# A 120-row piece of 88 columns half way through the run, moved by two transfers each way in place of five

## The chip, the cores and the metric

The kernel runs on one core of a Trainium2 chip. The metric is the device time of one execution in microseconds, over several executions. One core has no second die to compare with; all runs used here are of the state "fast". Several chips were used, and the kernel before was run again beside every experiment: it took between 477.96 and 481.73 us. Times are compared as ratios to the kernel before on the same chip.

## The reference, cut to what matters

```
x: (1, 512, 512, 192) bf16      w: (1, 1, 4, 48, 48) bf16
out[pixel, g, :] = x[pixel, g, :] @ w[0, 0, g]        # 4 groups of 48 channels
```

This is a grouped 1x1 convolution: 262,144 pixels of 384 bytes go in and as many come out, 201.3 MB in all. Each pixel is multiplied by four 48x48 matrices. There is little arithmetic for each byte.

## The kernel before

Pixels lie in SBUF, the memory on the chip, as columns: a column is one pixel in each of the 128 partitions ("rows"). Loads on the sync queue bring 80 columns at a time into a ring of 240 columns. PE (the matrix engine) transposes, VectorE copies what was transposed, PE multiplies it by the weights, ScalarE copies the result to an output ring of 280 columns, and stores on the scalar queue (q10 in the profile; the loads are q1) carry it out. Four columns are a "group".

The plan reckons with 8 rows for each of the 16 DMA engines in a transfer of 128 rows. The tail of the kernel before bears this out: the one engine that still works there moves eight packets of 6,144 bytes, then eight of 3,072, each packet one row of the last two stores (packet records, 475.4 to 478.2 us). One field of the plan is different: a piece of 120 rows, meant to give 15 engines 8 rows each and one nothing. It is there to relieve one DMA engine. Since 120 rows don't add up to a whole number of 128-row columns, a few columns of 16 rows stand beside it.

```python
FULL = (("sync", 0, 128, 128),)
PARTIAL = (                                   # queue, first row, rows, outer
    ("sync", 0, 16, 4), ("sync", 32, 16, 4),
    ("pool", 52, 44, 11), ("pool", 20, 12, 3), ("pool", 96, 32, 8),
)
REST = (("sync", 0, 16, 4),)
PARTIALS = ((72, PARTIAL), (4, REST))
FRONT_SLOTS = 9
FILL_BEFORE = (2, 3)
...
        # transfers(): a piece that is not of 128 rows
        view = px.rearrange("(c a i) n -> a c (i n)", a=outer, c=rows // outer)
        yield n, view, tile[r0:r0 + rows, at * C:(at + c1 - c0) * C]
...
            # gpsimd: a tiny transfer of 5 rows ("filler") ahead of two of the three blocks
            for p in partial:
                gp.wait_ge(t_done, freed(p))
                for n, dram, sbuf in transfers(xf, ring, p, ("pool",)):
                    filler(n)
                    gp.dma_start(sbuf, dram).then_inc(ld_sem[ld_key[p.i, n]], 16)
```

The outer number is meant to say over how many engines a block is dealt. In the packet records of the kernel before, at most 4 load packets of the 16-row blocks and at most 11 of the gpsimd blocks run at a time. The fillers are meant to keep the gpsimd blocks off the engine that is to be relieved; how they do so, no trace shows, only that one engine is idle beside the piece's store (next section).

## Time and profile before

| | before |
|---|---|
| time, median of the first 3 runs | 479.5 us (479.33 to 479.69) |
| span of the profiled run (first to last instruction) | 479.1 us |
| bytes moved | 201.75 MB, 421 GB/s over the span |
| DMA share (mean busy share of the 16 engines), 10 to 470 us | 0.98 to 1.03 in every 10 us |
| PE busy | 428.6 us |
| end of the DMA engines | 15 of them at 472.9 to 475.3 us, one at 478.2 us |

From the page of the kernel before: the busy time of the compute engines, the busy tenths of the DMA engines in 40 slices, and what they moved in each slice.

```profile
PE 428.6 (89%) x6178; PEld 387.1 (81%) x6178; DVE 246.9 (52%) x258; ACT 388.5 (81%) x515; POOL 7.0 (1%) x18
...
DMA  8999999999999999999999999999999999999995
GB/s 325 442 393 426 430 434 428 429 433 435 435 427 428 430 432 434 424 424 417 432 427 431 433 429 428 428 442 433 426 432 427 438 428 430 437 419 434 423 415 223
```

The DMA engines are full from the second slice to the last but one, at about 430 GB/s. PE is busy for 428.6 us and has slack. DMA is what bounds this kernel.

From the table of stages of the kernel before (the stretch; its length; busy us and count of PE, weight loads, VectorE, ScalarE and gpsimd; PE's granted clock; DMA share; GB/s):

```profile
180.00:190.00 10.00, 1.95 (x18) 1.97 (x19) 0.48 (x1) 0.00 (x0) 0.00 (x0) 0.60 1.02 440
...
230.00:240.00 10.00, 9.90 (x152) 9.02 (x149) 5.75 (x6) 8.82 (x13) 0.00 (x0) 1.00 0.99 417
472.00:475.30 3.30, 0.00 (x0) 0.00 (x0) 0.00 (x0) 0.00 (x0) 0.00 (x0) 0.51 0.49 201
475.30:478.30 3.00, 0.00 (x0) 0.00 (x0) 0.00 (x0) 0.00 (x0) 0.00 (x0) 0.50 0.06 25
```

In the first line PE waits for the 120-row piece and does nearly nothing, but DMA moves 440 GB/s: that wait costs no time. In the last line the DMA share is 0.06, one engine of 16, for 3 us.

From the waits (us in total, times, longest) and from the DMA issues (count, size, us from issue to landing) of the kernel before:

```profile
PE xT_ps L320 <- DMA ring<-in_x_dram: 15.7, 4, 10.4
...
ACT oring L416 <- DMA out_dram<-oring: 12.5, 6, 3.6
```

```profile
ring<-in_x_dram POOLq DMA_DIRECT2D x1, 864.0 KB, 45.7
...
out_dram<-oring POOLq DMA_DIRECT2D x1, 864.0 KB, 41.2
```

The trace also keeps a record of every DMA packet: its queue, its start, its duration and its bytes, though not its engine. Here one packet is one row of a transfer (23 loads of 128 rows and 80 columns left 2944 packets of 30,720 bytes). Packets of one size take the same time nearly always: 1138 ns for 80 columns (30,720 bytes), 1025 ns for 72 columns, 968 ns for 68. The first is 27 GB/s for one engine, the rate that the prediction reckons with. One unbroken chain of packets is slower: between 60 and 440 us its loads take 18 ns more and its stores 61 to 71 ns more. Picked out by their length alone, these are 145 of 2489 loads of 80 columns, about one in 17. Loads and stores together, 194 of the 271 that follow another of the kind begin within 5 ns of its end. So I take this chain for one engine of the 16, 4% slower than the rest over loads and stores together. It is the relieved one: while the piece's store keeps the other engines busy, at 221 to 224 us, 15.1 engines are busy on average in place of 16, and the slow packets are missing from the record just there.

### The profile page before, as it was taken

The page shows a single profiled execution, that of the slowest core. Times are in us where ns is not written, and L with a number is a line of the kernel's source. Part 1 is how long each engine was busy: PE and PEld are TensorE (multiplying, and loading weights), DVE is VectorE, ACT ScalarE, POOL GpSimd, SP SyncE. Part 2 cuts the span into 40 slices and gives each one's busy share as a digit, 9 for nine tenths or more (in the row PEclk, how much of TensorE's full clock was granted, in tenths as well). Part 3 has the DMA queues.
Part 4 walks back from the last instruction along what each step waited for, and adds up shares of the span by engine and source line. Part 5 has one row for each costly group of instructions (what it writes and reads, how often), then busy time and mean ns, then how long its engine had stood idle before and what let it go on. Part 6 is the DMA issues. An engine that isn't in the chain of part 4 may idle for free.

```text
span 479.1 us, 13570 instructions
## 1 busy us (share of the span) xinstructions
PE 428.6 (89%) x6178; PEld 387.1 (81%) x6178; DVE 246.9 (52%) x258; ACT 388.5 (81%) x515; POOL 7.0 (1%) x18
## 2 busy tenths in 40 slices
PE   5999999999999763989998999999999798899980
PEld 4888888888889753878888888888888687888870
DVE  2655556555555440545654555555556355355540
ACT  2998899988999771878898888999888696688881
POOL 1000000000020000020000000000000000000000
PEclk9999999999999995999999999999999899799997
DMA  8999999999999999999999999999999999999995
GB/s 325 442 393 426 430 434 428 429 433 435 435 427 428 430 432 434 424 424 417 432 427 431 433 429 428 428 442 433 426 432 427 438 428 430 437 419 434 423 415 223
DMA packets 9894, 201.75 MB, mean 421 GB/s; under 512 B 1657, under 2 KB 1817, under 8 KB 2457
## 3 DMA queue, kind: packets, MB, share of 16 engines
q1 hardware_dynamic: 4156, 98.25, 48.1%
q10 hardware_dynamic: 5100, 98.23, 48.0%
q0 software_dynamic: 608, 4.87, 2.4%
q8 instruction: 20, 0.33, 0.2%
q14 instruction: 10, 0.07, 0.0%
HBM read 100.68 MB, written 100.66 MB: 420 GB/s over the span
## 4 chain that ended last, share of the span: by engine, by line
PE 55%; DMA 29%; ACT 9%; issue 1%; ACTq 1%; POOL 1%; another core or an unknown queue 1%; SPq 0%
PE o_ps L340 32%; PE xT_ps L320 23%; DMA out_dram<-oring 18%; DMA ring<-in_x_dram 11%; ACT oring L416 9%; ACTq L397 1%; POOL fill L263 0%; POOL ring L270 0%; POOL out_dram L276 0%; SPq L289 0%; SPq L282 0%; ACTq L390 0%; ACTq L399 0%
## 5 line engine op out<-in xcount | busy, mean ns | idle before, releaser
L416 ACT CAST oring<-o_ps 128x768 bf16<-128x768 f32 x514 | 387.2, 801 | 79.7 <-PE o_ps L340 59.7
L379 DVE COPY xT_sb<-xT_ps 128x1536 bf16<-128x1536 bf16 x257 | 246.2, 958 | 215.9 <-PE xT_ps L320 215.9
L340 PE MATMUL o_ps<-wt,xT_sb 128*128 128x144 bf16 (+1 forms) x3084 | 288.2, 235 | 20.7 <-ACT oring L416 15.4
L340 PEld LDWEIGHTS o_ps<-wt,xT_sb 128*128 128x128 bf16 x3084 | 211.3, 99 | 59.2 <-ACT oring L416 49.6
L320 PE MATMUL xT_ps<-ident,ring 128*128 128x128 bf16 x3084 | 221.2, 222 | 15.7 <-DMA ring<-in_x_dram 15.7
L320 PEld LDWEIGHTS xT_ps<-ident,ring 128*128 128x128 bf16 x3084 | 189.2, 99 | 18.4 <-issue 13.9
L263 POOL DMA_DIRECT2D fill<-in_x_dram x4 | 2.4, 597 | 205.6 <-PE xT_ps L320 137.8
L301 PE MATMUL o_ps<-w_sb,esel 48*128 48x48 bf16 x10 | 0.6, 210 | 2.8 <-DMA w_sb<-in_w_dram 2.8
L301 PEld LDWEIGHTS o_ps<-w_sb,esel 48*128 48x128 bf16 x10 | 0.5, 112 | 2.8 <-issue 2.8
L372 DVE CAST wt<-o_ps 128x480 bf16<-128x480 f32 x1 | 0.7, 659 | 3.4 <-PE o_ps L301 3.4
L416 ACT ACT_TABLE_LOAD x1 | 1.3, 1283 | 0.8 <-PEq L436 0.8
L270 POOL DMA_DIRECT2D ring<-in_x_dram x3 | 1.7, 563 | 0.0
L276 POOL DMA_DIRECT2D out_dram<-oring x3 | 1.7, 558 | 0.0
L249 POOL TENSOR_SCALAR_AFFINE_SELECT esel<-esel 48x272 bf16<-48x272 bf16 x1 | 0.4, 404 | 0.0
L246 POOL MEMSET esel<- 48x272 bf16 x1 | 0.3, 318 | 0.3 <-POOLq L436 0.3
L253 POOL TENSOR_SCALAR_AFFINE_SELECT ident<-ident 128x128 bf16<-128x128 bf16 x1 | 0.3, 284 | 0.0
L247 POOL MEMSET ident<- 128x128 bf16 x1 | 0.2, 199 | 0.0
L436 POOL MEMSET const-float32-0.0<- 128x1 f32 x1 | 0.1, 99 | 0.3 <-issue 0.3
L436 POOL MEMSET const-bfloat16-1.0<- 128x1 bf16 x1 | 0.1, 102 | 0.0
L436 POOL MEMSET const-uint8-127<- 128x1 uint8 x1 | 0.1, 102 | 0.0
L436 POOL MEMSET const-float32-1.0<- 128x1 f32 x1 | 0.1, 99 | 0.0
## 6 DMA issues: line engine op xcount, KB each, us to landing
ring<-in_x_dram SPq DMA_DIRECT2D x23, 3840.0 KB, 27.2
out_dram<-oring ACTq DMA_DIRECT2D x13, 3456.0 KB, 40.6
out_dram<-oring ACTq DMA_DIRECT2D x11, 3264.0 KB, 39.3
out_dram<-oring ACTq DMA_DIRECT2D x3, 1344.0 KB, 22.4
out_dram<-oring ACTq DMA_DIRECT2D x2, 1920.0 KB, 21.9
out_dram<-oring ACTq DMA_DIRECT2D x1, 3072.0 KB, 31.8
ring<-in_x_dram SPq DMA_DIRECT2D x1, 2880.0 KB, 19.9
ring<-in_x_dram SPq DMA_DIRECT2D x1, 2304.0 KB, 10.9
```

The lines of the kernel that those rows point to most:

```text
L249: gp.affine_select(out=esel[:], in_=esel[:], pattern=[[-1, ECOLS]], compare_op=AluOpType.is_equal, fill=0.0, base=ESHIFT, channel_multipli ...
L263: gp.dma_start(dst, src).then_inc(fill_sem[k], 16)
L270: gp.dma_start(sbuf, dram).then_inc(ld_sem[ld_key[p.i, n]], 16)
L276: gp.dma_start(dram, sbuf).then_inc(st_sem[i][n], 16)
L301: last = pe.matmul(o_ps[:, NOB - 1, col:col + CG], lhsT=esel[:, s0:s0 + 128], rhs=w_sb[:, g, :], start=True, stop=True, skip_group_check=True)
L320: last = pe.transpose(xT_ps[:, g % NXP, j * 128:(j + 1) * 128], xg[:, j * 128:(j + 1) * 128], ident[:])
L340: last = pe.matmul(o_ps[:, v % NOB, c0_:c1_], lhsT=xs[:, j * 128:(j + 1) * 128], rhs=wt[:, WOFF[tc]:WOFF[tc] + (c1_ - c0_)], start=(tc == ...
L372: dve.tensor_copy(wt[:], o_ps[:, NOB - 1, 0:WCOLS]).then_inc(wc_sem, 1)
L379: dve.tensor_copy(xT_sb[pair % NXS][:, 0:n * 2 * UC].rearrange("p (g c) -> p g c", g=n), xT_ps[:, b0:b0 + n, 0:2 * UC]).then_inc(e_done[pa ...
L397: act.dma_start(dram, sbuf).then_inc(st_sem[i][n], 16)
L416: act.copy(out_columns(g).rearrange("p (u c) -> p u c", u=2), o_ps[:, v % NOB:v % NOB + 2, 0:UC]).then_inc(fa_done[g % (2 * NTOK)] if g < ...
L436: nc = _bacc.Bacc("TRN2", target_bir_lowering=False, num_devices=1)
```

## The change

The intent: give the slow engine still less work (88 columns in place of 72, by which 128-row columns go from 1980 to 1964), put the relief half way through the run, and move the piece by one gpsimd transfer of 88 rows and one of 32 rows on the sync queue (outward: on the scalar queue), in place of three and two. The plan of the ring is rewritten so that a piece of 88 columns fits; cut here.

```diff
-PARTIAL = (
-    ("sync", 0, 16, 4), ("sync", 32, 16, 4),
-    ("pool", 52, 44, 11), ("pool", 20, 12, 3), ("pool", 96, 32, 8),
-)
+PARTIAL = (("sync", 0, 32, 4), ("pool", 32, 88, 11))
 REST = (("sync", 0, 16, 4),)
-PARTIALS = ((72, PARTIAL), (4, REST))
-FRONT_SLOTS = 9
+FRONT_SLOTS = 12
+MIDDLE = ((12, REST), (60, FULL), (88, PARTIAL))
...
-FILL_BEFORE = (2, 3)
...
+        self.at = 4 * self.g0 % RCOLS
+        self.regular = self.full and size == BIG and self.at % BIG == 0
...
-            last = [q for q in pieces if q.slot == p.slot - SLOTS]
-            return -(-last[-1].g1 // 2) if last else 0
+            return max(0, -(-(4 * p.g1 - RCOLS) // 8))
```

More of the change, by code (lines that the diff above doesn't have):

```diff
@@ L39 @@
 FULL = (("sync", 0, 128, 128),)
-PARTIAL = (
-    ("sync", 0, 16, 4), ("sync", 32, 16, 4),
-    ("pool", 52, 44, 11), ("pool", 20, 12, 3), ("pool", 96, 32, 8),
-)
+PARTIAL = (("sync", 0, 32, 4), ("pool", 32, 88, 11))
 REST = (("sync", 0, 16, 4),)
-PARTIALS = ((72, PARTIAL), (4, REST))
-FRONT_SLOTS = 9
+FRONT_SLOTS = 12
+MIDDLE = ((12, REST), (60, FULL), (88, PARTIAL))
 FILL_ROWS = 5
-FILL_BEFORE = (2, 3)
-NFILL = 2 * len(FILL_BEFORE)
 class Field:
@@ L68, with __init__ @@
 class Piece:
-    def __init__(self, i, slot, at, field, c0, size):
-        self.i, self.slot, self.at, self.field = i, slot, at, field
+    def __init__(self, i, field, c0, size):
+        self.i, self.field = i, field
         self.c0, self.c1, self.size = c0, c0 + size, size
         self.g0, self.g1 = field.g0 + self.c0 // 4, field.g0 + self.c1 // 4
+        self.at = 4 * self.g0 % RCOLS
         self.full, self.blocks = field.full, field.blocks
+        self.regular = self.full and size == BIG and self.at % BIG == 0
         assert size % 4 == 0 and self.at + size <= RCOLS
@@ L85, in plan_fields @@
 def plan_fields(npix):
-    few = sum(cols * sum(b[2] for b in blocks) for cols, blocks in PARTIALS)
+    few = sum(cols * sum(b[2] for b in blocks) for cols, blocks in MIDDLE)
     front = sum(HEAD) + BIG * FRONT_SLOTS
@@ L90, in plan_fields @@
         cols = (npix - few) // 128 - front
-        parts = [(front, FULL), *PARTIALS]
+        parts = [(front, FULL), *MIDDLE]
     assert cols % 4 == 0
@@ L101, in plan_pieces @@
 def plan_pieces(fields):
-    pieces, slot, at = [], 0, 0
+    pieces = []
     for f in fields:
-        head = list(HEAD) if f is fields[0] and f.cols > sum(HEAD) else []
-        if f.full and at:
-            slot, at = slot + 1, 0
+        first = [f.cols]
+        if f.full:
+            first = list(HEAD) if not f.g0 and sum(HEAD) <= f.cols else []
         c = 0
         while c < f.cols:
-            n = head.pop(0) if head else min(BIG, f.cols - c)
-            if at + n > BIG:
-                slot, at = slot + 1, 0
-            pieces.append(Piece(len(pieces), slot, slot % SLOTS * BIG + at, f, c, n))
-            c, at = c + n, at + n
+            n = first.pop(0) if first else min(BIG, f.cols - c)
+            pieces.append(Piece(len(pieces), f, c, n))
+            c += n
     return pieces
@@ L130, in plan_stores @@
                 if ends and c >= f.cols - LATE_COLS:
-                    end = min(end, c + LATE_PART)
+                    end = min(OCOLS - at, LATE_PART) + c
                 end = min([end, f.cols] + [e for e in ends if e > c])
@@ L143, in loop_spans @@
     for p in pieces + [None]:
-        if p and p.full and p.size == BIG:
+        if p and p.regular:
             run.append(p)
@@ L195, in bass_standalone__grouped__vision_kernel @@
     for p in pieces:
-        part = sum(1 for q in pieces if q.slot == p.slot and q.i < p.i)
         for n in range(len(p.blocks)):
-            ld_key[p.i, n] = (p.slot % SLOTS, part) if p.full else ("partial", part, n)
+            ld_key[p.i, n] = (p.at // BIG,) if p.regular else ("piece", p.i, n)
     partial = [p for p in pieces if any(b[0] == "pool" for b in p.blocks)]
@@ L209, in bass_standalone__grouped__vision_kernel @@
         wt = es.enter_context(nc.sbuf_tensor("wt", [128, WCOLS], BF16))
-        fill = es.enter_context(nc.sbuf_tensor("fill", [FILL_ROWS, NFILL * 8], BF16))
+        fill = es.enter_context(nc.sbuf_tensor("fill", [FILL_ROWS, 16 * max(1, len(partial))], BF16))
         xT_ps = es.enter_context(nc.psum_tensor("xT_ps", [128, NXP, 1024], BF16))
@@ L226, in bass_standalone__grouped__vision_kernel @@
         go_sem = sem("go_sem")
-        fill_sem = [sem(f"fill{k}") for k in range(NFILL * len(partial))]
+        fill_sem = [sem(f"fill{k}") for k in range(2 * len(partial))]
         def columns(g):
@@ L256, in _, with filler @@
             used = []
-            def filler(n):
-                if n in FILL_BEFORE:
-                    k = len(used)
-                    src = xf[0:2 * FILL_ROWS, 0:4].rearrange("(t p) n -> p t n", t=2)
-                    dst = fill[:, 8 * k:8 * k + 8].rearrange("p (t n) -> p t n", t=2)
-                    gp.dma_start(dst, src).then_inc(fill_sem[k], 16)
-                    used.append(k)
+            def filler():
+                k = len(used)
+                src = xf[0:2 * FILL_ROWS, 0:4].rearrange("(t p) n -> p t n", t=2)
+                dst = fill[:, 8 * k:8 * k + 8].rearrange("p (t n) -> p t n", t=2)
+                gp.dma_start(dst, src).then_inc(fill_sem[k], 16)
+                used.append(k)
             for p in partial:
@@ L268, in _ @@
                 for n, dram, sbuf in transfers(xf, ring, p, ("pool",)):
-                    filler(n)
+                    filler()
                     gp.dma_start(sbuf, dram).then_inc(ld_sem[ld_key[p.i, n]], 16)
@@ L274, in _ @@
                         for n, dram, sbuf in transfers(of, oring, s, ("pool",)):
-                            filler(n)
+                            filler()
                             gp.dma_start(dram, sbuf).then_inc(st_sem[i][n], 16)
@@ L314, in transposes @@
                             pe.wait_ge(ld_sem[key], 16)
-                        todo += keys if p.full else []
+                        todo += keys if p.regular else []
                     xg = columns(g)
```

## The prediction

> What bounds the kernel now: DMA. The page's slices show the 16 DMA engines at 9 tenths or more from the second slice to the last but one, at about 430 GB/s; the table of stages has a DMA share of 0.98 to 1.03 in every 10 us between 10 and 470 us. PE is busy 428.6 of 479.1 us; its long wait (10.4 us, on the 120-row load, 45.7 us to landing) costs nothing: the DMA share stays at 1.0. What counts is the DMA engine that ends last, and lost engine time.
>
> The DMA packet records show one engine slower all the time. Row packets take 1138 ns (80 columns in) and 968 or 1025 ns (out) almost everywhere; one unbroken chain of packets takes about 18 ns more per load and 61 to 71 ns more per store, 4%, some 19 us over the run. The 120-row piece spares this engine 72 columns x 8 rows x 768 B = 442 KB, 16.4 us at 27 GB/s. That is not enough: in the tail 15 engines end between 472.9 and 475.3 us, and one works on alone until 478.2 (DMA share 0.49 in 472 to 475.3, then 0.06, one of 16).
>
> Balance after: columns of 128 rows go from 1980 to 1964, so the slow engine moves 16 x 8 x 768 B = 98 KB less, 3.6 us at 27 GB/s, 3.8 at its own rate. [...] Taken alone, the slow engine would end near 474.4 and the others between 473 and 476: 479.5 becomes about 477. The slow engine also stood idle for about 4 us near 220 to 224, beside the pool's store; the 60-column store ahead of the piece may fill some of that. Two added groups (1.7 us of PE) and the tail's new store sizes hardly matter. One pool DMA in place of three saves 2 us of issue and the hole between their packets (158 to 162 us); the load may land in 30 us, which shortens a PE stall that costs nothing.
>
> [...]
>
> [...] I predict 478.6 us, range 475.5 to 484.5; faster by over 2%: 0.01, within 2%: 0.95, slower by over 2%: 0.04.
>
> What would show it: the lone last engine gone from the tail (all end within 2.5 us); [...] DMA share 1.0 through the piece; PE's wait there below 10 us.
>
> What would make it wrong: the spared engine not being the slow one [...], slowness that belongs to partitions instead, [...] or idle DMA engines before the piece, since the slow engine falls up to 10 us behind at its later place.

Passages that no trace or run of this case shows are cut from the text above: its picture of which engine works in which rows, and how it worked out a cost from that. The sum came to this. The slow engine ends at 478.2 us, less 3.8 us, so at 474.4; the others, at 472.9 to 475.3 us before, end between 473 and 476, with a term in it (8 more columns of 16 rows, 25 KB more for each of four engines, estimate 0.9 us at the 27 GB/s of a packet). That gave 477 us if the new row layout costs nothing. A term for the layout, which was my guess and rested on no trace (3 to 7 us for each engine, with a probability of one half), made it 481 to 485 us. As signs, the text named gpsimd packets of 33.8 KB at 1.25 us if the layout is free, and at 1.5 to 2.5 us with slow ordinary packets beside them if not. The slow engine's lag of up to 10 us is an estimate too, 4% of the 240 us before its relief; so are the 20 and 18.2 us of spared work in the expectations of e8 to e10 (88 and 80 columns x 8 rows x 768 B at 27 GB/s).

## The result, and the profile after

Ratios are the mean time of one kernel's runs over that of the other's of the same rounds, so they are not quite the ratios of the medians quoted.

| | before | after |
|---|---|---|
| median | 479.6 us (479.33 to 480.2, 4 runs) | 493.59 us (492.02 to 494.38, 4 runs) |
| ratio | | 1.0286, 95% interval 1.0258 to 1.0314: slower |
| span profiled | 479.1 us | 491.5 us |
| GB/s over the span | 421 | 410 |

The page of the kernel after, the same lines:

```profile
PE 432.1 (88%) x6202; PEld 390.6 (79%) x6202; DVE 247.8 (50%) x259; ACT 390.1 (79%) x517; POOL 3.7 (1%) x12
...
DMA  8999999999999999999999999999999999999996
GB/s 320 440 397 431 436 425 432 425 439 430 434 426 433 431 433 435 431 428 314 312 400 428 424 431 357 355 390 415 425 425 433 428 436 430 433 429 432 423 419 256
```

The DMA line looks as it did. The GB/s line has two dents: 314 and 312 when the piece is loaded, 357, 355 and 390 when it is stored. The engines are as busy as ever and move a quarter less. The table of stages of the kernel after:

```profile
220.00:230.00 10.00, 6.51 (x81) 6.16 (x79) 3.01 (x4) 5.22 (x7) 0.00 (x0) 0.85 1.03 329
230.00:240.00 10.00, 9.85 (x147) 9.04 (x145) 5.62 (x7) 8.60 (x12) 0.00 (x0) 0.98 1.03 321
240.00:250.00 10.00, 8.66 (x128) 7.64 (x126) 5.13 (x6) 7.96 (x11) 0.00 (x0) 1.00 0.95 308
...
300.00:310.00 10.00, 9.91 (x151) 9.04 (x148) 5.91 (x7) 9.12 (x13) 0.00 (x0) 1.00 1.03 330
310.00:320.00 10.00, 1.78 (x28) 1.48 (x25) 1.75 (x2) 0.84 (x2) 0.00 (x0) 0.79 0.96 356
320.00:330.00 10.00, 2.34 (x21) 2.30 (x21) 0.04 (x1) 2.30 (x3) 0.00 (x0) 0.50 0.95 392
```

A DMA share of 1.03 at 321 GB/s says that packets take longer, not that engines wait. The last two lines show PE nearly idle. The waits and the issues say for what:

```profile
ACT oring L408 <- DMA out_dram<-oring: 36.3, 7, 15.8
...
PE xT_ps L312 <- DMA ring<-in_x_dram: 3.4, 2, 1.7
```

```profile
ring<-in_x_dram POOLq DMA_DIRECT2D x1, 2904.0 KB, 36.0
out_dram<-oring POOLq DMA_DIRECT2D x1, 2904.0 KB, 39.4
```

PE no longer waits for the piece's load (10.4 us before, 1.7 at most now). ScalarE waits for room in the output ring instead, 36.3 us in place of 12.5.

The packet records give the size of the loss. The "load phase" is the time from the first to the last gpsimd load packet of the piece, the "store phase" the same for its stores. A packet of undisturbed length is the reference for its size (1251 ns for the piece's 33,792 bytes). The means are those of the packets that begin in the phase: 27 loads in the load phase, 90 stores of 60 columns in the store phase.

| packets of the kernel after | undisturbed | mean in the load phase | mean in the store phase |
|---|---|---|---|
| gpsimd, the piece | 1251 ns | 1941 ns | 1628 ns |
| ordinary loads, 80 columns | 1138 ns | 1896 ns | 1148 ns |
| ordinary stores, 72 and 60 columns | 1025 and 855 ns | 1153 ns (72) | 1040 ns (60) |

Ordinary loads suffer when the piece is loaded and hardly when it is stored. Ordinary stores suffer more when it is stored. Summed over all packets, the time over the undisturbed time is 124 us of engine time in the load phase and 74 us in the store phase. Over 16 engines that is 7.8 and 4.7 us, against 0.1 and 0.5 us before: 11.9 us more, of a difference in span of 12.4 us. (Which packets at the edges of a phase are counted moves a figure of these sums, here and in the table below, by up to 1.6 us of engine time.)

### The profile page after: what moved, and what is told of

Read it like the earlier page. It is cut to its first block, busy times and chain, and to the rows that moved or that the text cites. A ratio compares the mean times of both kernels' runs of the same rounds, so it can differ in the third digit from the quotient of the medians.

```text
span 491.5 us, 13595 instructions
## 1 busy us (share of the span) xinstructions
PE 432.1 (88%) x6202; PEld 390.6 (79%) x6202; DVE 247.8 (50%) x259; ACT 390.1 (79%) x517; POOL 3.7 (1%) x12
## 4 chain that ended last, share of the span: by engine, by line
PE 66%; ACT 12%; DMA 11%; another core or an unknown queue 6%; issue 1%; ACTq 1%; SPq 0%
PE o_ps L332 38%; PE xT_ps L312 28%; ACT oring L408 12%; DMA out_dram<-oring 10%; ACTq L389 1%; DMA ring<-in_x_dram 1%; SPq L281 0%; SPq L274 0%; ACTq L382 0%; ACTq L391 0%
## 5 line engine op out<-in xcount | busy, mean ns | idle before, releaser
L332 PEld LDWEIGHTS o_ps<-wt,xT_sb 128*128 128x128 bf16 x3096 | 213.5, 99 | 83.3 <-ACT oring L408 74.4
L255 POOL DMA_DIRECT2D fill<-in_x_dram x2 | 1.2, 624 | 283.1 <-PE xT_ps L312 212.1
L262 POOL DMA_DIRECT2D ring<-in_x_dram x1 | 0.6, 584 | 0.0
L268 POOL DMA_DIRECT2D out_dram<-oring x1 | 0.6, 578 | 0.0
```

The lines of the kernel that those rows point to most:

```text
L255: gp.dma_start(dst, src).then_inc(fill_sem[k], 16)
L268: gp.dma_start(dram, sbuf).then_inc(st_sem[i][n], 16)
L332: last = pe.matmul(o_ps[:, v % NOB, c0_:c1_], lhsT=xs[:, j * 128:(j + 1) * 128], rhs=wt[:, WOFF[tc]:WOFF[tc] + (c1_ - c0_)], start=(tc == ...
```

## The experiments

The theory: the row layout costs the time. The old blocks have rows that cost nothing extra beside the 128-row transfers, the new ones don't. I had a picture of which engine works in which rows. The packet records name neither engine nor row, so no run shows it. What the runs can show is what a move of rows costs. ("Same engines" means the same outer numbers in the plan.) Rivals: the later place (the slow engine lags more before its relief), the 88 columns, or the single large gpsimd transfer.

The sums of the packet records for all runs, in us of engine time over the undisturbed time (gpsimd + sync queue + scalar queue):

| run | load phase | store phase | ratio to before (95%) |
|---|---|---|---|
| before | 0 + 0.1 + 1.2 | 2.1 + 3.2 + 2.4 | |
| after | 60.7 + 45.1 + 18.3 | 33.1 + 1.7 + 39.6 | 1.0286 (1.0258 to 1.0314) |
| e1_own_ports | 0.5 + 0.6 + 1.4 | 2.3 + 3.4 + 5.0 | 1.0013 (0.9983 to 1.0042) |
| e2_wide_in_before | 47.5 + 90.4 + 22.5 | 31.5 + 2.9 + 27.0 | 1.0285 (1.0247 to 1.0323) |
| e3_shift4 | 6.7 + 19.4 + 4.2 | 0.8 + 5.8 + 1.9 | 1.0105 (1.0075 to 1.0134) |
| e4_load_own | 0 + 1.4 + 1.9 | 46.0 + 4.5 + 35.9 | 1.0118 (1.0094 to 1.0142) |
| e5_store_own | 57.6 + 45.6 + 21.6 | 0 + 1.4 + 3.8 | 1.0174 (1.0142 to 1.0206) |
| e7_sync_shift4 | 0.2 + 5.7 + 2.6 | 0.2 + 3.1 + 11.2 | 1.0044 (1.0019 to 1.0070) |
| e12_pool36 | 52.4 + 30.0 + 14.9 | 41.3 + 1.5 + 29.6 | 1.0323 (1.0285 to 1.0362) |
| e13_double | 22.2 + 32.3 + 9.9 | 25.7 + 2.4 + 5.4 | 1.0137 (1.0115 to 1.0159) |

### e1: the kernel after with the old rows

```diff
-PARTIAL = (("sync", 0, 32, 4), ("pool", 32, 88, 11))
+PARTIAL = (
+    ("sync", 0, 16, 4), ("sync", 32, 16, 4),
+    ("pool", 52, 44, 11), ("pool", 20, 12, 3), ("pool", 96, 32, 8),
+)
+FILL_BEFORE = (2, 3)      # and filler(n) as in the kernel before
```

> The kernel after with one part undone: the 88-column piece keeps its place, its columns and the 12-column piece, but its rows are dealt out as before (five transfers[...]). Theory [...]: the slow packets go, piece packets take 1.25 us, GB/s stays at 430 through the piece, and the time is 475.5 to 479 us. Rival (the later place, the 88 columns, or the slow engine's lag before the piece cost it): still 488 us or more.

Measured: 480.85 us (479.85 to 481.72), ratio 1.0013: the loss is gone. The result is correct. Of the table of stages of e1:

```profile
220.00:230.00 10.00, 8.05 (x122) 7.31 (x120) 4.69 (x6) 7.62 (x11) 0.00 (x0) 1.00 1.00 427
230.00:240.00 10.00, 9.76 (x148) 8.86 (x145) 5.79 (x7) 9.18 (x13) 0.00 (x0) 1.00 0.99 423
...
300.00:310.00 10.00, 9.83 (x147) 8.81 (x145) 5.75 (x6) 8.80 (x13) 0.00 (x0) 1.00 1.02 427
...
468.00:470.00 2.00, 2.00 (x32) 1.80 (x29) 1.25 (x2) 1.71 (x3) 0.00 (x0) 1.00 0.71 291
472.00:474.00 2.00, 0.27 (x5) 0.06 (x2) 0.00 (x0) 1.27 (x2) 0.00 (x0) 0.98 0.67 278
474.00:476.00 2.00, 0.00 (x0) 0.00 (x0) 0.00 (x0) 0.00 (x0) 0.00 (x0) 0.50 0.98 398
```

427 and 423 GB/s stand where the kernel after had 329 and 321. So the old rows, in their five transfers, take the loss away, and neither the place nor the 88 columns is the cause. But e1 is not faster than before either, and a part of my expectation (475.5 to 479 us) missed. The last three lines show a hole in the tail: at 468 to 470 and 472 to 474 us a third of the engines have no store to do, then all 16 work, and they stop within 2 us of each other, the last at 477.2 us.

### e2: the kernel before with the new rows only

```diff
-PARTIAL = ( ...five blocks... )
+PARTIAL = (("sync", 0, 32, 4), ("pool", 32, 88, 11))
-FILL_BEFORE = (2, 3)
+FILL_BEFORE = (1,)
```

> The kernel before with only the row layout of the change: 72 columns at the old place, one sync transfer of 32 rows and one gpsimd transfer of 88 rows each way. Theory: 72/88 of the loss of the kernel after, so 488 to 493 us, with load packets of 1.3 to 2.2 us in place of 1.03 in the piece. Rival (place or columns): 479 to 480 us, as before.

Measured: 494.44 us (492.66 to 495.81), ratio 1.0285, a little above what was expected and the same as the whole change costs. The table of stages of e2, while the piece is loaded:

```profile
150.00:160.00 10.00, 7.64 (x116) 6.84 (x113) 4.97 (x6) 7.12 (x10) 0.00 (x0) 1.00 1.02 271
160.00:170.00 10.00, 8.06 (x86) 7.49 (x87) 2.87 (x3) 5.60 (x9) 0.00 (x0) 0.66 1.01 292
```

The engines are full and move 271 GB/s. With e1 this closes the circle: taking the layout away removes the loss, and the new layout, put into the kernel before, brings all of it. Both runs change the number of transfers and the fillers together with the rows; e3 separates these.

### e3: the gpsimd blocks four partitions lower

```diff
-    ("pool", 52, 44, 11), ("pool", 20, 12, 3), ("pool", 96, 32, 8),
+    ("pool", 48, 44, 11), ("pool", 16, 12, 3), ("pool", 92, 32, 8),
```

> The kernel before with its three gpsimd blocks four partitions lower: same transfers, same engines, same sizes, same HBM rows[...]. Theory [...]: slower by 3 to 9 us[...]. Rival (the number or size of gpsimd transfers, or the order of rows in HBM): no difference, 479 to 480 us.

Measured: 486.09 us (484.47 to 487.3), ratio 1.0105. The number and size of the transfers, the outer numbers and the HBM addresses are those of the kernel before; only SBUF partitions moved by 4, and 5 us were lost. That rules out the single large gpsimd transfer and the order of HBM rows as the sole cause. It also bounds what is shown: rows alone cost 5 us here and 6.3 us in e13 (further down), both with three gpsimd transfers. No run has the new rows in several transfers, so how much of the other 7 to 9 us of e2 comes from the wider layout, and how much from the single large transfer, is not shown. The packets that suffer most are the ordinary loads (19.4 us of engine time, against 6.7 us of the displaced gpsimd loads). Yet only 24 of 176 gpsimd packets are more than a tenth longer than they should be; in e2 it is 114.

### e4 and e5: one direction at a time

Each uses the old rows for one direction and the new ones for the other, in the kernel after. Rows land at wrong pixels, so both give a wrong result (relative error 0.27).

```diff
+        self.sblocks = self.blocks              # rows of the stores
+        if blocks is PARTIAL:                   # dealt out by OUTWARD instead
+            self.sblocks, pix = [], self.blocks[0][4]
+            for (queue, r0, rows, outer) in OUTWARD:
+                self.sblocks.append((queue, r0, rows, outer, pix))
+                pix += rows * cols
...
+PARTIAL, OUTWARD = OWN, WIDE                    # e4;  e5: WIDE, OWN
```

> The kernel after with the piece loaded in the old row layout and stored in the new one (wrong result on purpose: rows of the piece land elsewhere). Theory with separate directions (loads collide with loads, stores with stores): the slow load packets, 122 us of engine time or 7.6 us per engine, go; the stores' 5 us stay: 484 to 487 us, with 30720-byte loads at 1.14 us through the piece. Rival (the two directions share one rate): the loss is shared in equal parts, and the load phase of the kernel after would have slowed stores as much as loads, which its trace denies; no other number.

> The other half of e4: the piece is loaded in the new row layout and stored in the old one (wrong result on purpose). Theory (loads and stores collide apart, the two parts add up): slow load packets stay, the slow stores go, ratio to before about 1.017 (e1 to after lost 13 us, of which e4 gave back 8), 487 to 490 us. Rival (the load phase alone carries the loss through the waits that follow): as slow as the kernel after, ratio 1.028.

Measured: e4 486.15 us (485.02 to 486.31), ratio 1.0118; e5 488.09 us (486.66 to 490.22), ratio 1.0174. The two losses add up to 2.9%, the whole is 2.86%. The tables of stages, e4 first, then e5; the piece is loaded at 230 to 240 us and stored at 300 to 310 us:

```profile
230.00:240.00 10.00, 9.75 (x148) 8.89 (x146) 5.79 (x7) 9.08 (x12) 0.00 (x0) 1.00 1.00 427
...
300.00:310.00 10.00, 9.83 (x148) 8.87 (x146) 5.68 (x6) 8.80 (x13) 0.00 (x0) 1.00 0.98 342
```

```profile
230.00:240.00 10.00, 9.88 (x137) 9.06 (x136) 5.31 (x6) 8.12 (x12) 0.00 (x0) 0.92 1.02 317
...
300.00:310.00 10.00, 9.91 (x149) 8.95 (x147) 5.95 (x7) 9.00 (x12) 0.00 (x0) 1.00 1.01 426
```

The slow stretch follows the direction that has the new rows. In e4's store phase the loads lose 4.5 us of engine time and the stores, with the piece's own, 82. In e5's load phase the loads lose 103 us with the piece's own and the stores 22. So the directions are mostly separate, though not wholly in the load phase.

### e7 and e11: the same on the sync and scalar queues, and a control

```diff
-    ("sync", 0, 16, 4), ("sync", 32, 16, 4),
+    ("sync", 4, 16, 4), ("sync", 36, 16, 4),      # e7
+    ("sync", 32, 16, 4), ("sync", 0, 16, 4),      # e11
```

> The kernel before with its two 16-row blocks of the sync and scalar queues four partitions higher[...]; the gpsimd transfers are untouched. Theory [...]: the load packets of 27648 bytes on the sync queue, 1.025 us before, take 1.2 us or more on average, and the time grows by 0.5 to 3 us. Rival (only gpsimd transfers suffer): packets at 1.03 us, time unchanged.

> Control for e7: the kernel before with the two 16-row blocks of the sync and scalar queues exchanged, rows 32-47 first and rows 0-15 second. The partitions of each transfer change by 32[...]. Theory: no change, ratio 0.998 to 1.002, packets of 27648 bytes on the sync queue at 1.025 us. Rival (any departure from the old rows costs): as e7, ratio 1.004.

Measured: e7 482.87 us (481.13 to 483.76), ratio 1.0044. Its 32 displaced load packets take 1085 ns on average (1025 before, six of them clearly longer): the slowing was less than the 1.2 us that I had named, but the time grew as expected. e11 479.1 us (478.74 to 480.39), ratio 0.9985 (0.9961 to 1.0010), and all its 32 packets take 1025 ns. A step of 4 partitions costs something on the sync and scalar queues too (1.0044); the exchange in e11, a step of 32, costs nothing that can be measured (0.9985). So the loss doesn't come from every departure from the old rows, and it isn't peculiar to gpsimd's transfers. Why 32 is free and 4 is not, no run shows.

### e6, e8, e9, e10: where the gain of the better balance went

e1 should have gained 2.5 us. Its lone last engine was gone, so why no gain? My reading: ScalarE waited 12.2 us for the landing of the piece's store, late in the run, and PE could not catch up.

```diff
-FRONT_SLOTS = 12
+FRONT_SLOTS = 9        # e6;  e8: 6
```

> e1 with the piece three ring slots (240 columns) earlier, where the old piece was. In e1 no DMA engine was left alone in the tail any more, but the DMA engines had holes from 464 to 475 us, because the copies ended at 473.5 us in place of 469.0, after a wait of 12.2 us for the landing of the piece's store at 319 to 331 us. Theory (the late place leaves PE too little time to catch up, and hides the gain of the balance): 476 to 478.5 us where before is 479.5, ratio 0.993 to 0.998, the last store issued by 470 us. Rival (the balance of the engines gives nothing): ratio 1.000 to 1.004.

> e6 three more ring slots earlier. Theory of e6 carried on: the copies end as early as in e6 or earlier, but the spared engine gets 20 us of work less while it is only 3 to 6 us behind, so it stands idle for longer near the piece's store: 476 to 480 us, not better than e6 by more than 1 us. If the place doesn't matter at all: equal to e1.

Measured: e6 480.76 us (480.49 to 483.32), ratio 1.0021 (0.9998 to 1.0045); e8 482.9 us (482.14 to 483.86), ratio 1.0058 (1.0039 to 1.0077). My theory of the place fell. In e8 the copies do end early (last store issued at 468.2 us, in e1 at 473.5), but the relieved engine stands idle at 152 to 156 us and 185 to 190 us, and in the tail one engine is alone again until 480.2 us: the relief was wasted while there was nothing for it to do.

e9 and e10 cut the piece in two, at groups 129 and 329, e9 with 44 and 44 columns, e10 with 40 and 40:

```diff
-FRONT_SLOTS = 12
-MIDDLE = ((12, REST), (60, FULL), (88, PARTIAL))
+FRONT_SLOTS = 5
+MIDDLE = ((12, REST), (24, FULL), (44, PARTIAL), (720, FULL), (36, FULL), (44, PARTIAL))
...
-                gp.wait_ge(go_sem, 1)
+                gp.wait_ge(go_sem, turn + 1)
```

> The 88 columns of e1[...], but as two 120-row pieces of 44 columns, one at group 129 and one at group 329. Theory: e1, e6 and e8 lost the gain of the balance to idle time of the spared engine beside the piece (5 to 10 us of one engine) and to a wait of 12 us for the landing of the piece's store; half a piece gives half the lead and half the landing time, so no 1 us slice near the pieces below 15.7 busy engines, no wait for a store over 6 us, all engines ending within 2.5 us, and 476 to 478.5 us, ratio 0.992 to 0.998. Rival (the kernel before is at its floor, given the tail of PE): 479 to 481 us.

> As e9 with 40 and 40 columns, 80 in all, which spares the slow engine 18.2 us in place of 20 (before: 16.4): within 1 us of e9 if the sum is not the limit; the slow engine ending last by 1 us or more if it is.

Measured: e9 480.29 us (479.17 to 481.59), ratio 1.0002 (0.9982 to 1.0023); e10 480.22 us (479.4 to 481.05), ratio 1.0003 (0.9984 to 1.0021). The waits of ScalarE for a landing store, e1 and then e9:

```profile
ACT oring L414 <- DMA out_dram<-oring: 20.4, 5, 12.2
```

```profile
ACT oring L414 <- DMA out_dram<-oring: 13.9, 6, 4.8
```

The long wait is gone, the idle time beside the piece nearly so (one slice at 15.5 busy engines in e9, none in e10), no engine is alone in the tail, and still nothing is gained. The copies end at 471.3 us in e9, against 469.0 before, and the engines have holes between 466 and 471 us. The packet records also show more work on average: 475.4 us for each engine in e9 and 474.4 in e1 against 473.4 before. So the lone last engine of the kernel before was worth less than it looked: when it is removed, the end of the copies and the average work of the engines take its place. Why the copies end later without the long wait, I did not settle. None of these versions beats the kernel before.

### e12 and e13: why the loss was so large

e3 costs 5 us, the wide layout 14 us. I tried twice to explain this, and missed twice. Both theories rested on my picture of the rows.

```diff
-PARTIAL = (("sync", 0, 32, 4), ("pool", 32, 88, 11))
+PARTIAL = (("sync", 0, 32, 4), ("pool", 36, 88, 11))        # e12, in the kernel after
```

```diff
-    ("pool", 52, 44, 11), ("pool", 20, 12, 3), ("pool", 96, 32, 8),
+    ("pool", 84, 44, 11), ("pool", 20, 12, 3), ("pool", 52, 32, 8),   # e13, in the kernel before
```

> The kernel after with one number changed: the gpsimd block of 88 rows starts at partition 36 in place of 32[...]. [...] Theory [...]: the loss shrinks by a fifth to a half, ratio to before 1.014 to 1.023, the mean of the piece's gpsimd load packets below 1.8 us (1.94 in the kernel after). Rival [...]: unchanged, ratio 1.026 to 1.031, 1.9 to 2.0 us.

> The kernel before with the 44-row gpsimd block at partitions 84-127 and the 32-row block at 52-83; all sizes, engines and HBM rows as before, the same eight partitions left out. [...] Theory [...]: of the first 44 gpsimd load packets, 15 or more take over 1.13 us, of the second 44 fewer than that; the time grows by 2 to 6 us. Rival [...]: the second 44[...] have more slow packets.

Measured: e12 494.74 us (492.91 to 499.67), ratio 1.0323. The gpsimd load packets took 1846 ns on average in place of 1941, less of a fall than expected, and the time did not fall at all. e13 486.32 us (485.98 to 487.25), ratio 1.0137. Of its first 44 gpsimd load packets 23 took over 1.13 us, of the second 44 it was 31. My theory had asked for fewer in the second 44 than in the first, so it fell; the rival had asked for more. Why e3, with all 88 gpsimd rows moved by 4 partitions, slows only 21 of its 88 loads stays open.

## Why the prediction was wrong

The range was 475.5 to 484.5 us, and 493.6 us came out.

- *DMA bounds the kernel; PE's wait on the piece costs nothing.* Right. After, the DMA engines are as busy as before and the time follows their GB/s; PE's wait on the load shrank to 1.7 us at most and nothing was gained.
- *The new row layout may cost more than the gain*. Right, as far as the runs go: e3, e7 and e13, which move rows and nothing else, lose time (1.0105, 1.0044, 1.0137), and the control e11 does not (0.9985). e1 and e2 show that the new layout brings the whole loss, though not how it divides between the rows and the single large transfer. A probability of one half was too little.
- *The layout's cost, if there is one: a guess of 3 to 7 us for each engine* (it rested on no trace). This is the term that failed, by size. Measured: 11.9 us per engine more than before, 12.4 in all. The piece's own 120 packets, gpsimd and sync, lost 82 us of engine time in the load phase, 0.69 us each; in the store phase the piece's own packets lost 48 us, 0.40 us each. Together that is 8.1 us per engine, so 3 to 7 was too low even for what it counted. And the guess took only packets of the piece, but others were slowed as well: the ordinary packets beside the piece lost 42 us in the load phase and 27 us in the store phase, another 4.3 us per engine. With 11.9 us the prediction's 477 would have become 489; most of what is left to 493.6 is the gain in the next point, which did not come.
- *The better balance is worth 2.5 us, so 477 us if the layout costs nothing.* Wrong. With the loss removed, e1 takes 480.85 us where before takes 480.65, and e9 and e10 are no better. The lone last engine did vanish, as I had said it would. But the tail is limited by the end of the copies (471.3 us in e9, 469.0 before) and by the average work (475.4 us for each engine in e9, 473.4 before), both close behind the slow engine, and I had looked at the last engine only.
- *Idle engines before the piece, as the slow engine falls behind at its later place.* Not seen: the DMA share is 1.00 or above from 200 to 220 us in the kernel after. Beside the piece's store, though, one engine stands idle from 318 to 328 us (15 busy engines in the packet records; DMA share 0.95 to 0.96 above), against 221 to 224 us before. The prediction hoped that the 60-column store would fill some of this idle time; it grew, by some 6 us of one engine.
- *Gpsimd packets of 1.5 to 2.5 us with slow ordinary packets beside them, if the layout costs something; DMA share 1.0 through the piece.* Both seen (means of 1.94 and 1.63 us; ordinary loads 1896 ns in the load phase), the share apart from 0.95 to 0.96 in three of the stretches shown. The DMA share can't tell the two cases apart, as I had half implied: it is 1.03 at 321 GB/s.

## What to carry to other kernels

When a transfer covers less than 128 partitions, try which rows it takes, not only how many bytes it moves: here the old blocks cost nothing even in the kernel after (e1, ratio 1.0013), the same blocks 4 partitions lower cost 5 us in 480 (e3, 1.0105), and a tidier layout of the same bytes, in fewer transfers, cost 14 us (e2, 1.0285). The DMA share hid this (1.03 at 321 GB/s); compare the GB/s of the stage, and the length of packets of one size, with those of an undisturbed stage. Before working on the engine that ends last, see what ends next: here removing it gained nothing (e1, e9 and e10: 1.0013, 1.0002 and 1.0003).
